# Attention then mixture of depths: the tail scores move to second place in the slot, the squares are summed a slot later, and the gate rows go ahead of those sums

## The chip, the cores and the metric

One NeuronCore of a Trainium2 chip runs the whole program. The metric is the device time of one execution in microseconds (us). Each run below has a time, and the profiled execution also has a trace.

## The reference

The input is q, k, v of 8 batches, 12 heads, 448 tokens and 64 dimensions in float32, and a small mixture-of-depths layer behind the attention:

```
q_n = q / (norm(q) + 1e-6);  k_n = k / (norm(k) + 1e-6)
attn = softmax(q_n @ k_n.T / tau)            # tau = 0.1
x[b] = heads of (attn @ v) side by side      # 448 x 768
scores = x @ w_gate                          # one number per token
top = the 128 tokens of each batch with the largest scores
out = x;  out[top] += sigmoid(scores[top]) * (relu(x[top] @ w1) @ w2)
```

w1 is 768 x 1024 and w2 is 1024 x 768.

## The kernel before

**Pairs and slots.** Two heads make a pair, six pairs a batch, so there are N = 48 pairs. The loop `for i in range(N + 1)` has one slot for each pair. The schedule is manual: on each engine, instructions run in the order in which the program writes them, and the framework adds the waits. Tokens are cut into seven blocks of 64 for either head; keys are cut into three whole column groups for each head (c = 0, 1, 2) and one shared tail group (c = 3).

**What a slot does.** `scores(i, c)` multiplies into a PSUM tile `sc` (a pool of two tiles, each of two banks); `exps(i, c)` is the exponential of it on ACT. `pv_tails` and `pv` multiply the exponentials of the pair before with its values into `o_ps`; `pv_evac` divides by the sum and writes into `x_b`, the batch's x. `transposes(i+1)` brings the next pair's normalized q and k through PE into `qkT_ps`, and `qkT_copy` (DVE) copies them to SBUF: the next slot's scores read that copy. `scale(i+2)` (POOL) normalizes the pair after that into `qkn`, of which there is one, and `values(i+2)` casts its v.

**Norms.** `square(p)` (ACT) squares q and k of pair p, which arrive by DMA into one of four raw buffers; eight matmuls with the identity (`sum_pe`) fold the squares into the second bank of an `sc` tile, and `sum_dve` reduces them into `ss`. `norm_a` (three small ACT instructions) and `norm_b` (a DVE reciprocal) follow once for up to three pairs. Before, squares, their sums and the tail scores all lie in the last part of one slot: the tail scores use the first bank of the tile whose second bank holds the sums.

**Order before.** scores 0 and 1, `pv_tails`, `pv` | exps 0 and 1, squares | list D1 | `pv_evac` | lists A, D2 | scores 2, transposes, `qkT_copy` | sums on PE, scores 3, sums on DVE | exps 2 and 3, norms | list C, scale, values, list P2, list B.

**The second layer.** Its steps are put in lists by slot (`at(slot, where, ...)`). For batch b, from slot s = 6(b+1): `store_x` (two stores of x on the SP queue, and a casting DMA on the POOL queue that makes `xh`, x in bf16), four `gate` rows (DVE, x times w_gate with a running sum), `rank_prep` (POOL), `rank_rep` (PE), four `rank_count` rows and four `pick` (DVE), `select`, `gather` in two parts (PE, reads `xh`), `ffn1` and `ffn2` in two halves, and `scatter` (an indirect DMA that adds into out). `x_b` and `xh` have two buffers each, so batch b+2 writes where batch b was. The last batch's second layer runs behind the loop.

## Time and profile before

| what | value |
|---|---|
| times of the runs shown | 325.1 and 320.91 us, median 323.0 us |
| profiled execution | 323.22 us |
| its span, first to last instruction | 319.3 us |
| mean granted TensorE clock | 0.897 of full |
| 48 slots, tail exponential of slot 0 to that of slot 47 | 17.9 us to 285.6 us |
| stores of one batch's x, two transfers | 768 and 576 KB |

The span is what the trace shows; about 3.9 us of the profiled execution's time lie outside it. PE, DVE, ACT, POOL and SP are the engines; PEld is PE's weight load.

### The profile page before, as it was taken

What the parts mean: (1) busy time and instruction counts of PE and PEld (TensorE: products, weight loads), DVE (VectorE), ACT (ScalarE), POOL (GpSimd) and SP (SyncE); (2) the same over time, 40 slices, a digit from 0 to 9 for tenths busy, and PEclk for the clock granted to TensorE, in tenths of its full rate; (3) what the DMA queues carried; (4) which work ended last, traced back from release to release, by engine and by line L of the source; (5) the groups of instructions that cost most, each with busy time, mean ns of one, the idle gap of its engine ahead of it and who ended that gap; (6) DMA issues with size and microseconds to landing.
All of it is one profiled execution on the core that took longest, in us unless ns stands there. A gap on an engine that the chain in (4) does not pass through costs nothing.

```text
span 319.3 us, 10375 instructions
## 1 busy us (share of the span) xinstructions
PE 246.7 (77%) x4503; PEld 188.9 (59%) x4503; DVE 184.1 (58%) x476; ACT 206.8 (65%) x317; POOL 158.1 (50%) x183
## 2 busy tenths in 40 slices
PE   7678777769897886969798789877978789587370
PEld 7466545547765675647665677656756566464350
DVE  2334365585667573667557575767674767686120
ACT  4768998968786785667667688755865646452020
POOL 5542657753667352844558357725572437303201
PEclk9989999997999697987889799959995979699697
DMA  7899999999999699667959499949121570306533
GB/s 271 228 302 290 280 268 247 293 284 275 291 282 256 142 226 240 202 123 162 235 150 271 84 220 251 270 89 206 32 28 26 132 142 2 51 2 134 139 49 49
DMA packets 31805, 57.68 MB, mean 181 GB/s; under 512 B 2192, under 2 KB 27792, under 8 KB 30736
## 3 DMA queue, kind: packets, MB, share of 16 engines
q1 hardware_dynamic: 27216, 43.75, 51.5%
q0 software_dynamic: 4128, 12.58, 21.8%
q8 instruction: 35, 0.57, 0.8%
q10 hardware_dynamic: 416, 0.69, 0.6%
q14 instruction: 10, 0.08, 0.1%
HBM read 39.71 MB, written 14.16 MB: 169 GB/s over the span
## 4 chain that ended last, share of the span: by engine, by line
PE 41%; DVE 24%; ACT 17%; DMA 8%; issue 5%; SPq 2%; POOLq 1%; DVEq 0%; ACTq 0%
PE o_ps L316 9%; PE sc L276 7%; ACT expS L289 7%; DVE junk L350 6%; PE m_ps L461 5%; PE sc L200 5%; DMA qk_raw<-in_k_dram 5%; ACT sq L193 4%; PE m_ps L470 4%; ACT expS L292 4%; DVE junk L395 4%; DMA xh<-x_b 4%; DVE qkT L264 3%; DVE x_b L330 3%; PE qkT_ps L258 3%
## 5 line engine op out<-in xcount | busy, mean ns | idle before, releaser
L231 POOL TENSOR_TENSOR qkn<-qk_raw,rs 128x896 bf16<-128x896 f32 (+1 forms) x48 | 92.3, 1922 | 117.3 <-PE qkT_ps L258 94.0
L289 ACT ACTIVATE expS<-sc 128x896 bf16<-128x896 f32 x144 | 126.4, 913 | 26.9 <-PE sc L276 26.9
L276 PE MATMUL sc<-qkT 64*128 64x448 bf16 x288 | 51.9, 387 | 33.0 <-DVE qkT L264 24.6
L292 ACT ACTIVATE expS<-sc 128x448 bf16<-128x448 f32 x48 | 26.1, 543 | 47.6 <-DVE ss L206 47.1
L316 PE MATMUL o_ps<-vo,expS 128*128 128x65 bf16 x1152 | 49.2, 202 | 0.0
L193 ACT ACTIVATE sq<-qk_raw 128x896 bf16<-128x896 f32 x48 | 45.5, 951 | 2.7 <-DMA qk_raw<-in_k_dram 2.7
L276 PEld LDWEIGHTS <-qkT 64*128 64x128 bf16 x288 | 13.8, 95 | 52.2 <-DVE qkT L264 29.1
L316 PEld LDWEIGHTS <-expS 128*128 128x128 bf16 x1152 | 42.9, 103 | 2.9
L200 PE MATMUL sc<-sq,iden_b 128*128 128x112 bf16 x384 | 29.3, 226 | 12.6 <-ACT sq L193 12.6
L258 PEld LDWEIGHTS <-qkn 64*64 64x64 bf16 x1344 | 28.2, 117 | 15.6 <-issue 12.2
L258 PE MATMUL qkT_ps<-iden_b,qkn 64*64 64x64 bf16 x1344 | 34.3, 203 | 3.8 <-POOL qkn L231 1.9
L264 DVE COPY qkT<-qkT_ps 128x960 bf16<-128x960 bf16 x48 | 31.4, 655 | 8.2 <-PE qkT_ps L258 7.9
L330 DVE TENSOR_TENSOR x_b<-o_ps,rden 128x512 f32<-128x512 f32 x48 | 33.2, 691 | 1.7
L329 DVE RECIPROCAL rden<-o_ps 128x8 f32<-128x8 f32 x48 | 9.9, 207 | 41.2 <-PE o_ps L316 37.9
L350 DVE CUSTOM_DVE_ANT_0 junk<-x_b,wg_b 128x768 bf16<-128x768 f32 (+1 forms) x32 | 33.4, 1045 | 0.2
L200 PEld LDWEIGHTS <-iden_b 128*128 128x128 bf16 x384 | 24.2, 105 | 14.1 <-issue 12.1
L238 POOL CAST vo<-v_raw 128x448 bf16<-128x448 f32 x48 | 28.6, 598 | 0.0
L461 PEld LDWEIGHTS <-w_sb 128*128 128x128 bf16 x384 | 24.9, 104 | 5.1 <-issue 3.6
L461 PE MATMUL m_ps<-xeT,w_sb 128*128 128x128 bf16 x312 | 22.2, 233 | 3.0 <-issue 2.4
L395 DVE SCALAR_TENSOR_TENSOR junk<-m_ps,own,tie 128x448 bf16<-128x448 f32 (+1 forms) x32 | 21.9, 683 | 0.8
L485 POOL DMA_INDIRECT out_dram<-oe,idx x8 | 13.0, 1630 | 18.6 <-DVE oe L435 8.8
L221 DVE RECIPROCAL rs<-rs 128x42 f32<-128x42 f32 (+2 forms) x18 | 7.0, 387 | 24.7 <-ACT rs L216 20.3
(83 smaller groups left out, 278.6 us busy)
## 6 DMA issues: line engine op xcount, KB each, us to landing
qk_raw<-in_q_dram SPq DMA_DIRECT2D x15, 672.0 KB, 4.8
qk_raw<-in_k_dram SPq DMA_DIRECT2D x15, 672.0 KB, 14.3
out_dram<-x_b SPq DMA_DIRECT2D x8, 768.0 KB, 10.8
xh<-x_b POOLq DMA_DIRECT2D x8, 768.0 KB, 12.4
v_raw<-in_v_dram SPq DMA_DIRECT2D x30, 192.0 KB, 11.4
out_dram<-x_b SPq DMA_DIRECT2D x8, 576.0 KB
v_raw<-in_v_dram SPq DMA_DIRECT2D x30, 144.0 KB, 8.7
w_sb<-in_moe_w_dram POOLq DMA_DIRECT2D x2, 1536.0 KB, 21.3
```

The source lines that it names most:

```text
L193: nc.scalar.activation(sq_tiles[p], raw[gi % NRAW][0][:, :, g].rearrange("p a b d -> p a (b d)"), AF.Square)
L200: nc.tensor.matmul(out=dst, lhsT=iden_b, rhs=sq[:, :, s * D8:(s + 1) * D8], start=(s == 0), stop=(s == Dh // D8 - 1))
L231: eng.tensor_mul(kn[:, :, b0:b1], qk[:, :, g, b0:b1], rs[:, m, :, b0:b1].rearrange("p a (b o) -> p a b o", o=1) .to_broadcast([P, 2, b1 - ...
L258: nc.tensor.transpose(out=qkT_ps[r, o:o + T], in_=kn[r, a, s], identity=iden_b[r, r], tile_position=(u * T, u * T))
L264: nc.vector.tensor_copy(qkT_tiles[p], qkT_ps[:, :W])
L276: nc.tensor.matmul(out=sc[:, u, :S], lhsT=qkT[r, KO + c * P:KO + (c + 1) * P], rhs=qkT[r, :S], start=True, stop=True, tile_position=(u * D ...
L289: nc.scalar.activation(ex[:, 2 * c:2 * c + 2], sc[:, :, :S], AF.Exp, scale=inv_tau)
L292: nc.scalar.activation(ex[:, TAIL], sc[:, 0, :S], AF.Exp, scale=inv_tau)
L316: nc.tensor.matmul(out=o_ps[:, u, j * E:(j + 1) * E], lhsT=ex[:, 2 * c + u, qc(j)], rhs=vo[:, u * NS + c], start=False, stop=(c == NC - 1) ...
L330: nc.vector.tensor_mul(x_tiles[b][:, :, 2 * hp * Dh:2 * (hp + 1) * Dh] .rearrange("p j (u d) -> p j u d", u=2), o[:, :, :, :Dh], rden.to_b ...
L350: nc.vector.tensor_tensor_reduce(out=junk[:, d0:d1], in0=x_tiles[b][:, j, d0:d1], in1=wg_b[:, d0:d1], scale=1.0, scalar=0.0 if prev is Non ...
L461: nc.tensor.matmul(out=ps[:, f * CAP:(f + 1) * CAP], lhsT=w1_sb[:, t, fc * P:(fc + 1) * P], rhs=xeT[:, t], start=(t == 0), stop=(t == KD - 1))
```

## The change

The slot's order becomes: list P1 | scores 0, `pv_tails` | scores 3 together with the PE sums of the squares made in the *last* slot | exps 0 and 3, this slot's squares | list D1 | sums on DVE, some norms | `pv`, `pv_evac` | list A | scores 1, exps 1, scores 2, exps 2, transposes, `qkT_copy` | scale, values, lists P2 and C, the other norms, list D3, list B. So four `sc` tiles are still taken in a slot, in another order. Squares are made six pairs ahead instead of five, with three buffers for `sq`.

Gate rows move from D2, behind `pv_evac`, to D1, ahead of the sums. Two of four `rank_count` rows and all four `pick` go from ahead of `qkT_copy` to D3, behind it. Most steps of the second layer start one slot later. `store_x` no longer makes `xh`: `half_x` does, five slots later (four and three for batches 5 and 6), at the slot's start.

At the end, slot 48 is no longer a loop pass: the last pair's `pv` stands behind the loop. The last pair's x goes into a tile of its own, `x_last`; `half_x` for the other five sixths of the last batch is issued in slot 47, and ACT casts the last sixth. `gather` part 1 and both `ffn1` halves of batch 6 run there too. At the start, the loads of group 3's q and k go ahead of the v loads of group 2 on the SP queue. `xeT` and `hT` become separate tiles for each half.

The core of the diff:

```
-    for gi in range(3):
-        load(gi, 2, nc.sync)
+    load(0, 2, nc.sync)
+    load(1, 2, nc.sync)
+    load(3, 0, nc.sync)
+    load(3, 1, nc.sync)
+    load(2, 2, nc.sync)
+    load(3, 2, nc.sync)
...
+    def half_x(b, d1=D):
+        xh_tiles[b] = xp.tile([P, NS, D], BF16, name="xh")
+        nc.gpsimd.dma_start(out=xh_tiles[b][:, :, :d1], in_=x_tiles[b][:, :, :d1])
...
+    late = dict(gate=(1, 2, 3, 4), rep=5, half=5, rank=6, select=7,
+                ffn=((8, "B"), (9, "B"), (10, "B"), (11, "A")))
+    mid = dict(late, ffn=((8, "B"), (9, "A"), (9, "B"), (10, "A")))
+    early = dict(gate=(1, 1, 2, 3), rep=4, half=4, rank=5, select=6,
+                 ffn=((7, "B"), (8, "A"), (8, "B"), (9, "A")))
+    last = dict(gate=(1, 1, 2, 2), rep=3, half=3, rank=4, select=5, ffn=())
...
+        at(s, "P2", store_x, b)
         for j in range(NS):
-            at(s + m["gate"][j], "D2", gate, b, j)
-        at(s + m["prep"], "P2", rank_prep, b)
+            at(s + m["gate"][j], "D1", gate, b, j)
+        at(s + m["gate"][3], "P2", rank_prep, b)
+        at(s + m["half"], "P1", half_x, b)
...
+        run(i, "P1")
+        sq = SQ.get(i - 1, [])
+        scores(i, 0)
+        if prev:
+            pv_tails(i - 1)
+        sc = ps_sc.tile([P, 2, 512], FP32, name="sc")
+        scores(i, 3, sc)
+        sums(sq, sc)
+        exps(i, 0)
+        exps(i, 3)
+        for p in SQ.get(i, []):
+            square(p)
+        run(i, "D1")
+        sums_dve(sq, sc)
+        norms(sq, i, True)
+        if prev:
             pv(i - 1)
-        if live:
-            exps(i, 0)
-            exps(i, 1)
-            for p in SQ.get(i, []):
-                square(p)
-        run(i, "D1")
-        if prev:
             pv_evac(i - 1)
         run(i, "A")
-        run(i, "D2")
...
+        scores(i, 1)
+        exps(i, 1)
+        scores(i, 2)
+        exps(i, 2)
         if nxt:
             transposes(i + 1)
             qkT_copy(i + 1)
-        if live:
-            sc = ps_sc.tile([P, 2, 512], FP32, name="sc")
-            sums(SQ.get(i, []), sc, lambda: scores(i, 3, sc))
-            exps(i, 2)
-            exps(i, 3)
-            norms(SQ.get(i, []))
-        run(i, "C")
         if i + 2 < N:
             scale(i + 2)
             values(i + 2)
         run(i, "P2")
+        run(i, "C")
+        norms(sq, i, False)
+        run(i, "D3")
...
         run(i, "B")
...
+    gather(b, 1, "A", True)
+    store_x(bb, x_last, 5 * P, D)
...
+    ffn1(b, 0, "A", True)
+    rank_prep(bb, True)
     ffn1(b, 1, "A", True)
-    rank_prep(bb)
+    nc.scalar.activation(xh_last, x_last, AF.Copy)
+    rank_rep(bb)
```

## Rows read from the trace of the kernel before

**Rows 1.** Slots 29-34, 35-40, 41-46: length, busy PE, PEld, DVE, ACT, POOL; clock, DMA.

```profile
170.30:202.70 32.40, 27.81 (x552) 21.55 (x551) 22.03 (x57) 25.07 (x38) 19.23 (x21) 0.95 0.86 201
202.70:240.90 38.20, 30.08 (x556) 22.74 (x555) 27.13 (x70) 25.12 (x38) 22.16 (x23) 0.90 0.55 111
240.90:279.80 38.90, 30.76 (x529) 22.80 (x527) 25.00 (x58) 21.89 (x35) 16.83 (x18) 0.81 0.35 68
```

**Rows 2.** Waits over the span: total us, times, longest us.

```profile
ACT expS L292 <- DVE ss L206: 47.1, 43, 3.6
PE sc L276 <- DVE qkT L264: 24.6, 13, 3.7
PE sc L200 <- ACT sq L193: 12.6, 28, 1.2
```

**Rows 3.** Timeline of a slot with rank rows (slot 29), DVE and PE.

```profile
175.40 0.84 DVE L403 TENSOR_SCALAR sel<-iota_r,rank 128x128 bf16<-128x128 bf16 x4
176.27 0.66 DVE L264 COPY qkT<-qkT_ps 128x960 bf16<-128x960 bf16 x1
...
176.98 0.36 PE L276 MATMUL sc<-qkT 64*128 64x448 bf16 x2 [2.43 <-DVE qkT L264]
```

**Rows 4.** Timeline of ACT, tail exponentials of slots 4, 5, 6, 28 and 29.

```profile
38.02 0.54 ACT L292 ACTIVATE expS<-sc 128x448 bf16<-128x448 f32 x1 [0.33 <-DVE ss L206]
42.16 0.54 ACT L292 ACTIVATE expS<-sc 128x448 bf16<-128x448 f32 x1 [0.33 <-DVE ss L206]
47.05 0.54 ACT L292 ACTIVATE expS<-sc 128x448 bf16<-128x448 f32 x1 [0.33 <-DVE ss L206]
...
170.27 0.54 ACT L292 ACTIVATE expS<-sc 128x448 bf16<-128x448 f32 x1 [0.63 <-DVE ss L206]
177.14 0.54 ACT L292 ACTIVATE expS<-sc 128x448 bf16<-128x448 f32 x1 [2.57 <-DVE ss L206]
```

**Rows 5.** The chain that ended last, in order of time: start, us, what.

```profile
15.29 7.01 DMA qk_raw<-in_k_dram
22.39 0.96 ACT sq L193
...
289.17 11.57 DMA xh<-x_b
300.79 2.75 PE sc L447 x24
```

**Rows 6.** Timeline of PE through slot 32, which has one ffn1 half.

```profile
187.98 0.55 PE L276 MATMUL sc<-qkT 64*128 64x448 bf16 x4
...
191.00 0.55 PE L200 MATMUL sc<-sq,iden_b 128*128 128x112 bf16 x8 [0.63 <-ACT sq L193]
...
191.58 1.50 PE L461 MATMUL m_ps<-xeT,w_sb 128*128 128x128 bf16 x24
193.01 0.55 PE L276 MATMUL sc<-qkT 64*128 64x448 bf16 x4
```

**Rows 7.** Gate rows: their source line (ns min/median/max), and one beside POOL's scale.

```profile
L350 DVE CUSTOM_DVE_ANT_0 junk<-x_b,wg_b x32: 682/948/2320, 45.1 to 281.1; 128x768 bf16<-128x768 f32 x28, 128x512 bf16<-128x512 f32 x4
251.02 1.93 POOL L231 TENSOR_TENSOR qkn<-qk_raw,rs 128x896 bf16<-128x896 f32 x1 [3.40 <-PE qkT_ps L258]
...
251.44 2.32 DVE L350 CUSTOM_DVE_ANT_0 junk<-x_b,wg_b 128x768 bf16<-128x768 f32 x1
```

**Rows 8.** Timeline behind the loop: eight gather matmuls in slot 47, the last pick.

```profile
283.79 0.61 PE L447 MATMUL m_ps<-sel,xh 128*128 128x128 bf16 x8
...
296.66 0.26 DVE L403 TENSOR_SCALAR sel<-iota_r,rank 128x128 bf16<-128x128 bf16 x1
```

**Rows 9.** Timeline of POOL's rank_prep in slot 27, its first and last instruction.

```profile
166.17 1.04 POOL L358 TENSOR_TENSOR diag<-iden_x,gate 128x512 f32<-128x512 f32 x1
...
168.22 0.19 POOL L367 CAST sg<-r 128x4 bf16<-128x4 f32 x1
```

**Rows 10.** The casting DMA's source line: issue to landing of its eight, min/median/max.

```profile
DMA to landing us min/median/max: 8.5/12.4/14.1
```

More of the change, by code (lines that the diff above doesn't have):

```diff
@@ L321 @@
     x_tiles = {}
+    x_last = const.tile([P, NS, P], FP32)
+    xh_last = const.tile([P, NS, P], BF16)
     def pv_evac(i):
@@ L358, in rank_prep @@
         nc.gpsimd.tensor_mul(
-            diag, iden_x,
-            g.rearrange("p (j o) -> p j o", o=1).to_broadcast([P, NS, P]))
+            diag[:, :2 if split else NS], iden_x[:, :2 if split else NS],
+            g[:, :2 if split else NS].rearrange("p (j o) -> p j o", o=1)
+            .to_broadcast([P, 2 if split else NS, P]))
+        if split:
+            for j in (2, 3):
+                nc.scalar.activation(diag[:, j], iden_x[:, j], AF.Copy,
+                                     scale=g[:, j:j + 1])
         sg = moe.tile([P, NS, 3], BF16, name="sg")
@@ L440, in gather @@
         sel, xh = st[b]["sel"], xh_tiles[b]
-        if part == 0:
-            st[b]["xeT"] = moe.tile([P, KD, CAP], BF16, name="xeT")
         t0, t1 = ((0, cut), (cut, KD))[part]
+        xe = moe.tile([P, t1 - t0, CAP], BF16, name=f"xeT{part}_{t1 - t0}")
+        st[b].setdefault("xeT", []).extend(xe[:, t] for t in range(t1 - t0))
         ps = bank(big)
         for t in range(t0, t1):
+            src = xh if not (b == B - 1 and t == KD - 1) else xh_last
+            d0 = 0 if src is xh_last else t * P
             for j in range(NS):
                 nc.tensor.matmul(out=ps[:, (t - t0) * CAP:(t - t0 + 1) * CAP],
-                                 lhsT=xh[:, j, t * P:(t + 1) * P], rhs=sel[:, j],
+                                 lhsT=src[:, j, d0:d0 + P], rhs=sel[:, j],
                                  start=(j == 0), stop=(j == NS - 1))
-        evac(eng, st[b]["xeT"][:, t0:t1].rearrange("p t c -> p (t c)"),
-             ps[:, :(t1 - t0) * CAP], AF.Copy)
+        evac(eng, xe.rearrange("p t c -> p (t c)"), ps[:, :(t1 - t0) * CAP], AF.Copy)
     def ffn1(b, part, eng="D", big=False):
         xeT = st[b]["xeT"]
-        if part == 0:
-            st[b]["hT"] = moe.tile([P, KF, CAP], BF16, name="hT")
+        h = moe.tile([P, 4, CAP], BF16, name=f"hT{part}")
+        st[b].setdefault("hT", []).extend(h[:, t] for t in range(4))
         ps = bank(big)
@@ L498, in run @@
             fn(*args)
-    late = dict(gate=(0, 1, 2, 3), prep=3, rep=4, rank=5, select=6, gather=7,
-                ffn=((7, "B"), (8, "B"), (9, "B"), (10, "A")), scatter=10)
-    mid = dict(late, ffn=((7, "B"), (8, "A"), (8, "B"), (9, "A")), scatter=9)
-    early = dict(gate=(0, 0, 1, 2), prep=2, rep=3, rank=4, select=5, gather=6,
-                 ffn=((6, "B"), (7, "A"), (7, "B"), (8, "A")), scatter=8)
-    last = dict(gate=(0, 0, 1, 1), prep=1, rep=2, rank=3, select=4, gather=5,
-                ffn=((5, "B"),), scatter=None)
+    late = dict(gate=(1, 2, 3, 4), rep=5, half=5, rank=6, select=7,
[4 more added lines that the diff above has]
+    last = dict(gate=(1, 1, 2, 2), rep=3, half=3, rank=4, select=5, ffn=())
     for b in range(B - 1):
@@ L521 @@
         at(s + m["select"], "B", gather, b, 0)
-        at(s + m["gather"], "A", gather, b, 1)
+        if b < B - 2:
+            at(s + m["select"] + 1, "A", gather, b, 1)
         for (d, w), (fn, n) in zip(m["ffn"], ((ffn1, 0), (ffn1, 1), (ffn2, 0), (ffn2, 1))):
             at(s + d, w, fn, b, n)
-        if m["scatter"]:
-            at(s + m["scatter"], "P2", scatter, b)
+            if fn is ffn2 and n == 1:
+                at(s + d, "P2", scatter, b)
     bb = B - 1
@@ L529 @@
     gb = const.tile([P, NS], FP32)
+    gc = const.tile([P, NS], FP32)
     for j in range(NS):
-        at(N - 2, "D2", gate, bb, j, 0, 4 * P, None, ga)
-        at(N - 1, "D2", gate, bb, j, 4 * P, 5 * P, ga, gb)
-    for b in range(B - 1):
-        at(HP * (b + 1), "P2", store_x, b)
+        at(N - 3, "D1", gate, bb, j, 0, 2 * P, None, ga)
+        at(N - 1, "D1", gate, bb, j, 2 * P, 4 * P, ga, gb)
+        at(N - 1, "D3", gate, bb, j, 4 * P, 5 * P, gb, gc)
+    at(N - 1, "P2", half_x, bb, 5 * P)
+    at(N - 1, "P2", store_x, bb, None, 0, 5 * P)
     at(3, "D1", load_wg)
@@ L549, in warm, with sums, sums_dve, norms @@
                              start=True, stop=True)
-    def sums(ps, sc, tail=None):
+    def sums(ps, sc):
         for m, p in enumerate(ps):
             sum_pe(p, sc[:, 1, m * SW:(m + 1) * SW])
-        if tail:
-            tail()
+    def sums_dve(ps, sc):
         for m, p in enumerate(ps):
             sum_dve(p, sc[:, 1, m * SW:(m + 1) * SW])
-    def norms(ps):
+    def norms(ps, i=None, early=None):
         for p in ps:
             n, g = nplace[p]
-            if g == NORMS[n][1] - 1:
+            if g == NORMS[n][1] - 1 and (i is None or early == (NORMS[n][0] == i + 2)):
                 norm_a(n)
@@ L583 @@
     values(1)
-    for which in range(3):
-        load(3, which, nc.sync)
     for i in range(N + 1):
@@ L658 @@
     ps = [bank(True), bank(True)]
-    for h in range(2):
-        for n in range(2):
-            ffn2_mm(bb, n, ps[n], h * 4, h * 4 + 4)
+    ffn2_mm(bb, 0, ps[0], 0, KF)
+    ffn2_mm(bb, 1, ps[1], 0, KF)
     ffn2_evac(bb, 0, ps[0], "A")
```

56 lines of the change are left out of this document (25 added, 31 removed).

## Prediction

> **What bounds the kernel now.** I read the stretches first, for which engine is full; then the waits, for what stops it; then the timeline of single slots. In the undisturbed stretch of six slots PE is busy 27.8 of 32.4 us, ACT 25.1, DVE 22.0 [rows 1]. None is full, so the slot is a chain that goes round the engines with PE as its longest part. The reader is to see that three waits recur [rows 2]: the tail exponential waits for the sums' reduction on DVE (43 of 48 slots, 47.1 us), the scores wait for the copy of q and k (24.6 us in 13 waits), and the sums wait for the squares (12.6 us in 28). The first is no bound by itself: it is ACT's idle time, and the scores ask for little more. The second is PE's and dear: in slot 29, which has the rank rows, the picks and then the copy stand on DVE one behind the other, and PE waits 2.43 us [rows 3]. That slot lasts 6.87 us, 170.27 to 177.14 [rows 4]. Behind the loop, the chain is one transfer: 11.57 us of casting DMA, then the gather [rows 5].
>
> Slots without the second layer are short: 4.14 us from 38.02 to 42.16, and 4.89 to 47.05 when the norms' three small instructions follow [rows 4].
>
> **The change, part by part.** Every gain is counted against the profiled execution: 323.2 us, of which 319.3 are its span. It lies 0.2 us above the median of the runs, so I take nothing off for that.
>
> *Start.* The k load issued at 15.29 landed at 22.30, and a square stood waiting until 22.39 [rows 5]. Its issue stood behind twelve v loads; four of them now come after it. Four twelfths of the 15.3 us before it are at most some 4 us of earlier issue, and behind the load stands ACT, which has its own work until close to then. I take 2 us; ends 0 and 4.
>
> *Light slots (2 to 10).* The sums no longer wait for the squares of their own slot, but the transposes are now the last PE work, so that the copy lies open: 0.66 us [rows 3] plus two hand-overs. PE's own work for a slot follows from slot 32: 193.01 − 187.98 = 5.03, less 0.63 of waiting for the squares, less the ffn1 half (1.43 from its start at 191.58 to the next scores) leaves 2.97 [rows 6]. So 2.97 + 0.66 + about 0.4 of hand-overs = 4.0 us, against 4.14 and, every third slot, 4.89, where part of the norms comes under the copy. I take 0.2 us a slot, nine slots: 2 us; ends −1 and 4. This is the first place where a wait takes the other's place: the copy's for the square's.
>
> *Slots with the second layer, batches 0 to 3 (slots 11 to 34).* In a rank slot two rank rows and all picks go behind the copy. PE's 2.43 us of waiting then shrinks to the copy's own 0.71, which stays open as nothing else is on PE: 1.7 us for a batch [rows 3]. The spilled DVE work (the picks alone 0.84) lies in the next slot beside scores and pv. The squares' wait is 12.6 / 28 = 0.45 us [rows 2], four such slots a batch: 1.8 us. Against it, the second score pair's tile is free only when the sums are reduced, and this now stands behind a gate row (0.95, [rows 7]): walked by hand through slot 32, the reduction ends 0.3 us after PE wants the tile. So 4 × 0.15 = 0.6 us remain. Together 2.3 us a batch, 9.2 in four; ends 1.0 and 3.5 a batch.
>
> *Slots 35 to 40.* They take 38.2 us where the undisturbed six take 32.4 [rows 1]. Two of them are rank slots: 3.4 us. In the gate slot a second row met POOL's scale and took 2.32 instead of 0.95 us right ahead of the copy; ahead of the sums it has PE's pv as cover. With that and the squares' 0.6, I take 5.4; ends 3.4 and 7.
>
> *Slots 41 to 46.* 38.9 us at a clock of 0.81, PE busy 30.8 [rows 1]. The gate rows go two to a slot here, with the same collision (row at 251.44, [rows 7]), and one rank slot follows. One ffn1 half also goes behind the loop. PE's busy time is what it can't go below, so at most 8 us; the rank slot and two blocked rows are 1.7 + 2 × 1.4 = 4.5. I take 6; ends 3 and 8.
>
> *Behind the loop.* The big transfer leaves one slot earlier and is five sixths as long: issued some 4.6 us before 289.17, 9.6 us long, it lands near 294.2. Then the last pick is late next: 296.66 + 0.26 = 296.9 [rows 8]. The gather started at 300.79 [rows 5], so 3.9 us. The two ffn1 halves, ffn2 and gather part 1 of batch 6 fill what was idle, so PE comes to the gather without a pause: eight such matmuls took 0.61 at the higher clock [rows 8], 24 would be 1.8 in place of 2.75 us, 0.9 more. Two of four diag blocks move to ACT, beside POOL: nothing, as the two run at once. I take 5; ends 2 and 6.
>
> Gains: 2 + 2 + 9.2 + 5.4 + 6 + 5 = 29.6 us.
>
> *What is added: x's buffer.* `half_x` reads x_b five slots later than before, and batch b+2's first `pv_evac` writes the same buffer two slots after it. On POOL the transfer stands behind scale, values and rank_prep (166.17 to 168.41, 2.2 us [rows 9]), so it leaves near the end of the transposes of its slot, about 10 us ahead of that write by clean slot lengths. Landings took 8.5 to 14.1 us, median 12.4 [rows 10], all with 1.4 MB of stores beside them that now went five slots before. Behind the waiting `pv_evac` on DVE stands the q and k copy, and for that PE waits. So 0 to 4 us in each of five batches (0 to 4); I take 1, nearer the short end for the missing stores: 5 us; ends 0 and 20.
>
> *Loads a slot earlier.* Squares need q and k one slot sooner while buffers come free at the same time. Only the start showed ACT waiting for them. I take 1.5 us; ends 0 and 4. Three `sq` buffers, separate xeT and hT halves: nothing, and they take waits away at most; what covers them is PE's order. `half_x` and the stores stand past nothing on SP that waits; the scatter goes one slot later on POOL beside idle time.
>
> *Gate rows against POOL.* At the slot's start POOL runs scale and values; in the middle, where the rows were, it mostly waits for transposes. A row begun inside scale ended 0.8 us after scale did (251.44 + 2.32 against 251.02 + 1.93, [rows 7]): it stood still until scale was through. In slots with an ffn half, DVE's evacuation comes first and the row starts about when scale ends. So I take 1 us in all; the far end is the rival below.
>
> The Trainium skill, "SBUF — State Buffer", section "Who interferes with whom", says that a DVE instruction with two SBUF inputs and a GpSimd instruction that reads SBUF take turns on one port pair and the second blocks in full. This trace agrees: 2.32 us in place of 0.95. It speaks against moving the rows to where scale runs; by it alone the rival's sum holds.
>
> Costs 7.5, so 323.2 − 29.6 + 7.5 = 301.1: **301 us**.
>
> **The rivals.**
>
> *Buffer wait in full* (0.15). Every `pv_evac` two slots after `half_x` waits 4 us: five times 4 in place of 1 is 301 + 15 = 316. For it: the median landing is longer than the 10 us available, and DMA is busy through the first batches. Against: the stores are gone from beside it.
>
> *The wait only moves* (0.13). The reduction gates the second score pair as it gated the tail exponential, and the open copy eats the rest; only the start and the end gain: 323 − 7 = 316. For it: both waits lie on the same `sc` tile, and DVE's order decides both. Against: two rank rows and four picks really leave the copy's way.
>
> *Gate rows on the path* (0.12, slower). Each full row starts inside scale, and the sums, the second score pair, the transposes and the copy follow it. Extra 1.37 us (2.32 − 0.95), 28 rows [rows 7]: 38 us, or 301 + 38 = 339; where 0.3 us a row stays covered, 331. It decides once the blocked row ends later than pv and the first score pair do. For it: scale starts when transposes end and DVE is free 0.7 us later. Against: in ffn slots DVE first waits for the ffn half.
>
> **How the numbers follow.** The forecast has 0.60, with its own range 289 to 311: the low end takes the gains with no cost (293.6) and a third of what their upper ends (43.0 in all) add to 29.6; the high end gives up ten of the 18 us that lie between the gains taken and their lower ends (11.4 in all). The range 289 to 318 adds most of both rivals at 316 and leaves out the slower one and the outskirts. Two per cent (about what a measurement here can tell from none) are below 316.5 or above 329.5. Faster: 0.60, half of each rival at 316: 0.74. Same: the other halves, 0.14. Slower: 0.12.
>
> **What would show it.** In the trace after: the tail exponential starts right behind the first, with no wait for the reduction; the sums don't wait for squares; the rank slots take about 5 us; scores wait for the copy some 0.7 us in slots without an ffn half. If the buffer rival holds, `rden` or `x_b` on DVE waits for the casting DMA in the slots 13, 19, 25, 31 and 37. If gate rows do, many of 28 show 2.3 us and the second scores wait for the reduction. Behind the loop, the gather waits for the last pick and not for a DMA. The prediction is wrong if PE's waits for DVE grow by more than the copy's.

## The result and the profile after

The changed kernel takes 287.97 us (two runs, 287.29 and 288.65) against 323.0 us: 0.892 of the time before, 95% interval 0.865 to 0.918. Run again later it took 290.56 us, 0.908 (0.896 to 0.920). The forecast of 301 us had the direction and lies 13 us too high; its range began at 289, so the time is 1 us under it.

The profiled execution took 288.65 us, 1.8 us of it outside its span of 286.9. The trace of before is not that of the execution of 323.22 us: the record gives that one a span of 321.4 us at a clock of 0.892, and the trace has 319.3 at 0.897. So 1.8 us lie outside the span before as well, not 3.9, and the two traces are 32.4 us apart where the medians are 35.0 apart. First the page's head and the busy time of each engine in the whole span, before and then after.

```profile
span 319.3 us, 10375 instructions
...
PE 246.7 (77%) x4503; PEld 188.9 (59%) x4503; DVE 184.1 (58%) x476; ACT 206.8 (65%) x317; POOL 158.1 (50%) x183
```

```profile
span 286.9 us, 10402 instructions
...
PE 230.8 (80%) x4503; PEld 174.2 (61%) x4503; DVE 181.3 (63%) x482; ACT 208.4 (73%) x322; POOL 150.7 (53%) x183
```

The reader is to see that PE runs the same 4503 matmuls in 15.9 us less, at a granted clock of 0.957 instead of 0.897. Its idle time went from 319.3 − 246.7 = 72.6 to 56.1 us, 16.5 less. So the span's 32.4 us are half waits and half the same work done in less busy time.

The stretches below run from the first exponential of slot 11, 17, 23, 29, 35, 41 and 47 to the next of them. Columns as in [rows 1].

```profile
65.64:96.84 31.20, 27.32 (x545) 20.90 (x544) 21.30 (x56) 24.83 (x39) 17.01 (x21) 0.89 1.06 278
96.84:126.17 29.33, 26.79 (x553) 20.05 (x552) 22.03 (x58) 25.02 (x39) 18.04 (x22) 1.00 0.94 223
126.17:157.07 30.90, 27.88 (x553) 20.96 (x552) 22.02 (x58) 25.13 (x39) 17.33 (x22) 0.94 0.93 221
157.07:187.80 30.73, 27.18 (x552) 20.06 (x550) 22.34 (x58) 25.03 (x38) 18.08 (x22) 1.00 0.94 221
187.80:220.72 32.92, 28.86 (x565) 21.21 (x564) 23.07 (x61) 25.46 (x38) 19.56 (x28) 1.00 0.62 135
220.72:252.75 32.03, 25.39 (x521) 18.54 (x520) 24.69 (x67) 20.79 (x34) 18.43 (x21) 1.00 0.53 101
```

The table has the same marks in the trace before, each the timeline's start of a slot's first exponential, and splits each gain into PE's idle and PE's busy time:

| stretch | before: us, PE busy | after: us, PE busy | gain | of it PE idle | PE busy | forecast, before costs |
|---|---|---|---|---|---|---|
| start to slot 11 | 66.14, 49.78 | 65.64, 47.35 | 0.5 | −1.9 | 2.4 | 4 |
| slots 11 to 34, batches 0 to 3 | 137.51, 116.51 | 122.16, 109.17 | 15.4 | 8.0 | 7.3 | 9.2 |
| slots 35 to 40 | 37.76, 29.54 | 32.92, 28.86 | 4.8 | 4.2 | 0.7 | 5.4 |
| slots 41 to 46 | 41.41, 32.12 | 32.03, 25.39 | 9.4 | 2.7 | 6.7 | 6 |
| slot 47 and behind the loop | 36.48, 18.75 | 34.15, 20.04 | 2.3 | 3.6 | −1.3 | 5 |
| span | 319.3, 246.7 | 286.9, 230.8 | 32.4 | 16.5 | 15.9 | 29.6 (less 7.5 of costs) |

So the middle gave 30 us and both ends nearly nothing. No stretch of six slots is over 32.9 us now, and PE's granted clock is 1.00 in four of six. Before, two of the four stretches in slots 11 to 34 were long, and slots 41 to 46 too, all at a low clock:

```profile
98.61:135.08 36.47, 29.97 (x558) 22.78 (x556) 22.27 (x58) 25.23 (x39) 19.21 (x21) 0.86 0.85 209
135.08:171.20 36.12, 30.73 (x558) 23.62 (x556) 22.52 (x58) 25.24 (x39) 18.83 (x21) 0.86 0.78 192
...
241.41:282.82 41.41, 32.12 (x546) 24.21 (x547) 27.95 (x66) 22.30 (x37) 16.83 (x18) 0.81 0.33 64
```

PE's busy time in the first two was 30.0 and 30.7 us at 0.86, and is 26.8 and 27.9 at 1.00 and 0.94, for nearly as many matmuls. Slots 41 to 46 went from 32.1 us (0.81) to 25.4 (1.00); one ffn1 half left them too.

The waits of after, of those that [rows 2] lists and what answers to them:

```profile
DVE ss L210 <- ACT expS L296: 24.5, 14, 3.4
...
PE sc L280 <- DVE qkT L268: 15.6, 14, 3.5
...
PE sc L280 <- DVE ss L210: 7.2, 12, 0.9
...
ACT expS L296 <- PE sc L204: 5.1, 7, 1.3
```

The tail exponential no longer waits for the reduction (47.1 us before) but in seven cases for the sums on PE; the sums' wait for the squares (12.6 us) is gone from the list. The first is now the other way round: the reduction waits for the tail exponential (24.5 us, DVE's idle time), and PE for the reduction, 7.2 us in 12 waits. All of PE's waits for DVE together even rose, from 29.5 to 36.4 us; those for ACT fell from 21.0 to 4.3 and those for a DMA from 6.6 to 1.4 (sums over the view's lines).

A slot that has the spilled rank rows and picks reads as follows (timeline, DVE and PE).

```profile
105.63 0.66 DVE L268 COPY qkT<-qkT_ps 128x960 bf16<-128x960 bf16 x1 [0.18 <-PE qkT_ps L262]
106.35 0.36 PE L280 MATMUL sc<-qkT 64*128 64x448 bf16 x2 [0.76 <-DVE qkT L268]
...
107.66 0.81 DVE L416 TENSOR_SCALAR sel<-iota_r,rank 128x128 bf16<-128x128 bf16 x4
...
108.38 0.95 DVE L358 CUSTOM_DVE_ANT_0 junk<-x_b,wg_b 128x768 bf16<-128x768 f32 x1
...
109.37 0.28 DVE L210 TENSOR_REDUCE ss<-sc 128x14 f32<-128x112 f32 x1
...
109.70 0.37 PE L280 MATMUL sc<-qkT 64*128 64x448 bf16 x2 [0.60 <-DVE ss L210]
...
110.72 0.65 DVE L268 COPY qkT<-qkT_ps 128x960 bf16<-128x960 bf16 x1
```

The copy comes 0.18 us behind the transposes, and PE waits 0.76 us for it, not 2.43 [rows 3]. The picks, the gate row and the reduction then pass one behind the other while PE has tail products, scores and pv, and the reduction is late by 0.60 us. From copy to copy the slot takes 110.72 − 105.63 = 5.09 us; the rank slot before took 6.87 [rows 4]. Some executions of each kernel are disturbed and longer, so the ratios below are of undisturbed ones alone and the medians of all, and the profiled executions of e4, e7 and e8, which were disturbed, are used only where another run shows the same.

### The profile page after: what moved, and what is told of

The parts are those of the page before. It is cut to its first block, busy times and chain, and to the rows that moved or that the text cites. A ratio compares the mean times of both kernels' runs of the same rounds, so it can differ in the third digit from the quotient of the medians.

```text
span 286.9 us, 10402 instructions
## 1 busy us (share of the span) xinstructions
PE 230.8 (80%) x4503; PEld 174.2 (61%) x4503; DVE 181.3 (63%) x482; ACT 208.4 (73%) x322; POOL 150.7 (53%) x183
## 3 DMA queue, kind: packets, MB, share of 16 engines
q0 software_dynamic: 4512, 12.45, 24.5%
## 4 chain that ended last, share of the span: by engine, by line
PE 41%; DVE 21%; ACT 16%; DMA 10%; issue 7%; POOL 2%; SPq 1%; POOLq 1%; DVEq 0%; ACTq 0%
ACT expS L293 8%; PE sc L280 8%; DMA qk_raw<-in_k_dram 6%; PE o_ps L320 6%; PE m_ps L483 5%; DVE junk L408 5%; PE qkT_ps L262 5%; DVE junk L358 4%; DMA xh<-x_b 4%; PE sc L204 4%; PE m_ps L475 4%; ACT sq L197 3%; PE m_ps L462 3%; PE sc L285 3%; POOL qkn L235 2%
## 5 line engine op out<-in xcount | busy, mean ns | idle before, releaser
L235 POOL TENSOR_TENSOR qkn<-qk_raw,rs 128x896 bf16<-128x896 f32 (+1 forms) x48 | 80.7, 1681 | 101.0 <-PE qkT_ps L262 44.0
L280 PE MATMUL sc<-qkT 64*128 64x448 bf16 x288 | 49.3, 368 | 28.8 <-DVE qkT L268 15.6
L320 PE MATMUL o_ps<-vo,expS 128*128 128x65 bf16 x1152 | 46.3, 197 | 0.0
L268 DVE COPY qkT<-qkT_ps 128x960 bf16<-128x960 bf16 x48 | 31.4, 655 | 12.5 <-PE qkT_ps L262 12.5
L262 PEld LDWEIGHTS <-qkn 64*64 64x64 bf16 x1344 | 25.4, 111 | 15.8 <-issue 11.0
L358 DVE CUSTOM_DVE_ANT_0 junk<-x_b,wg_b 128x768 bf16<-128x768 f32 (+1 forms) x32 | 33.3, 1040 | 0.2
L262 PE MATMUL qkT_ps<-iden_b,qkn 64*64 64x64 bf16 x1344 | 30.8, 196 | 2.1 <-POOL qkn L235 2.1
L242 POOL CAST vo<-v_raw 128x448 bf16<-128x448 f32 x48 | 32.0, 668 | 0.0
L210 DVE TENSOR_REDUCE ss<-sc 128x14 f32<-128x112 f32 x48 | 12.7, 272 | 29.6 <-ACT expS L296 24.5
L204 PE MATMUL sc<-sq,iden_b 128*128 128x112 bf16 x384 | 28.0, 222 | 0.0
L475 PEld LDWEIGHTS <-w_sb 128*128 128x128 bf16 x384 | 22.3, 99 | 3.2 <-issue 2.2
L498 POOL DMA_INDIRECT out_dram<-oe,idx x8 | 13.0, 1628 | 14.5 <-DVE oe L448 7.0
L475 PE MATMUL m_ps<-xeT,w_sb 128*128 128x128 bf16 x288 | 18.1, 219 | 1.6 <-DVE xeT L446 1.6
```

The costliest lines, as they stand in the source:

```text
L204: nc.tensor.matmul(out=dst, lhsT=iden_b, rhs=sq[:, :, s * D8:(s + 1) * D8], start=(s == 0), stop=(s == Dh // D8 - 1))
L235: eng.tensor_mul(kn[:, :, b0:b1], qk[:, :, g, b0:b1], rs[:, m, :, b0:b1].rearrange("p a (b o) -> p a b o", o=1) .to_broadcast([P, 2, b1 - ...
L242: nc.gpsimd.tensor_copy(vo_bufs[p % NB][:, :, :Dh], raw[gi % NRAW][1][:, g])
L262: nc.tensor.transpose(out=qkT_ps[r, o:o + T], in_=kn[r, a, s], identity=iden_b[r, r], tile_position=(u * T, u * T))
L280: nc.tensor.matmul(out=sc[:, u, :S], lhsT=qkT[r, KO + c * P:KO + (c + 1) * P], rhs=qkT[r, :S], start=True, stop=True, tile_position=(u * D ...
L320: nc.tensor.matmul(out=o_ps[:, u, j * E:(j + 1) * E], lhsT=ex[:, 2 * c + u, qc(j)], rhs=vo[:, u * NS + c], start=False, stop=(c == NC - 1) ...
```

## The experiments

Each ran beside the kernel before, whose median in these jobs was 318.9 to 321.7 us. "Six slots" is the shortest of the four batches 0 to 3, from the start of one pair's transposes to that of the sixth pair after it (pairs 12 to 18, 18 to 24, 24 to 30, 30 to 36, read off the timeline). It is the clean batch, free of a pause or a late load. "Pairs 0-5", "5-12" and "41-47" are the time between those pairs' transposes. PE busy and clock are those of the span, and "at 0.50" is the time in it for which the granted clock was at its lower level, 1.2 GHz.

| run | median, us | ratio, 95% | pairs 0-5 | 5-12 | six slots | 41-47 | PE busy | clock | at 0.50, us |
|---|---|---|---|---|---|---|---|---|---|
| before | 323.0 | | 26.9 | 31.4 | 32.45 | 42.0 | 246.7 | 0.897 | 66 |
| after | 287.97 | 0.892 (0.865-0.918) | 30.1 | 28.5 | 29.33 | 31.9 | 230.8 | 0.957 | 24 |
| e1 | 312.86 | 0.972 (0.962-0.983) | 28.8 | 30.5 | 31.84 | 40.7 | 241.5 | 0.906 | 59 |
| e2 | 309.96 | 0.968 (0.957-0.978) | 28.2 | 31.4 | 32.23 | 33.5 | 239.1 | 0.944 | 35 |
| e3 | 320.52 | 1.000 (0.994-1.006) | 29.3 | 30.0 | 31.67 | 42.3 | 243.8 | 0.901 | 62 |
| e14 | 314.99 | 0.988 (0.981-0.995) | 28.7 | 30.5 | 32.94 | 35.7 | 239.7 | 0.902 | 61 |
| e5 | 301.53 | 0.952 (0.944-0.959) | 31.5 | 28.1 | 32.28 | 33.2 | 237.9 | 0.910 | 55 |
| e6 | 294.39 | 0.931 (0.919-0.942) | 28.7 | 29.9 | 28.67 | 33.3 | 235.7 | 0.935 | 38 |
| e10 (after again) | 290.56 | 0.908 (0.896-0.920) | 31.4 | 28.1 | 29.32 | 31.6 | 235.8 | 0.930 | 40 |

**One part alone in the kernel before.** e1: the tail exponentials go ahead of the reduction.

```
+    def sums_dve(ps, sc):
         for m, p in enumerate(ps):
             sum_dve(p, sc[:, 1, m * SW:(m + 1) * SW])
...
             exps(i, 2)
             exps(i, 3)
+            sums_dve(SQ.get(i, []), sc)
             norms(SQ.get(i, []))
```

> The kernel before with one swap: the third and the tail exponential are issued ahead of the sums' reduction on DVE, so that the tail exponential can't wait for it (47.1 us of waiting in the trace of before). Theory A (the prediction's: that wait is idle time of ACT and bounds nothing but light slots): 0.3 us in some nine light slots and little more, 317 to 323 us. Rival (the wait sits on the chain in most slots, as the next slot's second score pair needs that tile): 0.3 to 0.7 us in 43 slots, 295 to 310 us.

The tail exponential lost its wait for the reduction (it now waits 8.1 us for scores, 16 times) and the time fell by 2.8%. Yet the copy's wait is where it was, and the reduction now waits for the exponential, as in after:

```profile
PE sc L276 <- DVE qkT L264: 24.8, 14, 3.7
DVE ss L206 <- ACT expS L292: 21.1, 26, 4.4
```

A clean batch is 0.6 us shorter; the four batches together (pairs 12 to 36) take 131.9 us for 137.5, most of it out of the two long stretches. Neither side fits: the prediction's "no bound by itself" allowed little more than nothing, and its rival 0.3 to 0.7 us in 43 slots.

e2: two rank rows and the picks go behind the copy.

```
-            at(s + m["rank"], "D1" if j < 2 else "D2", rank_count, b, j)
+            at(s + m["rank"], "D1" if j < 2 else "D3", rank_count, b, j)
...
-            at(s + m["rank"], "D2", pick, b, j)
+            at(s + m["rank"], "D3", pick, b, j)
...
         norms(SQ.get(i, []))
+        run(i, "D3")
```

> The kernel before with two of the four rank rows and the four picks of each of seven batches moved behind the copy of q and k. Theory A (the prediction's price): 1.7 us in each of seven rank slots, 12 us, so about 311 us. Rival (a stall of 2.4 us also lowers the clock of the slots behind it, and the slot after it is long as well): 2.5 to 3.5 us each, 298 to 306 us. Against both: the work only moves to the next slot's reduction, 320 to 325 us.

3.2% faster, but nearly all of it at the end: pairs 41 to 47 fell from 42.0 to 33.5 us, where the two rank slots went from 8.01 to 4.98 and from 7.78 to 4.39. A clean batch gained 0.2 us: the rank slot is 0.9 shorter, the next 0.9 longer. There the selection on PE, early in the slot, waits for the picks that moved into it:

```profile
PE sc L276 <- DVE qkT L264: 9.8, 7, 2.4
...
PE m_ps L412 <- DVE sel L403: 7.6, 6, 1.5
```

So the same move was worth 3.0 and 3.4 us at the end of the loop and nothing in the steady part: the 1.7 us of the forecast fits neither.

e3: squares one slot earlier, summed in the next.

```
-        sq_tiles[p] = prep.tile([P, 2, NB7 * Dh], BF16, name="sq")
+        sq_tiles[p] = prep.tile([P, 2, NB7 * Dh], BF16, name="sq", bufs=3)
...
-        SQ.setdefault({3: 0, 4: 0, 5: 1, 6: 1}.get(p, p - 5), []).append(p)
+        SQ.setdefault({3: 0, 4: 0, 5: 1, 6: 1, 7: 2, 8: 2}.get(p, p - 6), []).append(p)
...
-            sums(SQ.get(i, []), sc, lambda: scores(i, 3, sc))
+            sums(SQ.get(i - 1, []), sc, lambda: scores(i, 3, sc))
...
-            norms(SQ.get(i, []))
+            norms(SQ.get(i - 1, []))
```

> The kernel before with the squares made one slot earlier and summed in the slot after, in the old order of the slot. Theory A: it takes away the sums' wait for the squares, 12.6 us in 28 slots, part of which something else takes over: 310 to 317 us. Rival (PE's wait for the squares only stands in for its wait for the copy): 320 to 324 us.

The wait for squares is gone, and no time with it. A clean batch gained 0.8 us (the forecast had 0.6), but the copy's wait rose from 24.6 to 29.2 us, scores wait for exponentials, and the start took 29.3 us instead of 26.9:

```profile
PE sc L276 <- DVE qkT L264: 29.2, 13, 3.7
...
PE sc L276 <- ACT expS L289: 8.0, 12, 2.8
```

e4 puts the three edits into the kernel before together, in its old order.

> The three edits of the runs beside it together in the kernel before: exponentials ahead of the reduction, squares a slot earlier, two rank rows and the picks behind the copy; slot order, gate rows, the casting transfer and the end stay. If the gain of the whole change comes from these waits, this has most of its 32 us apart from the end's 2 to 3: 293 to 300 us. If it comes from the new slot order itself (tail scores second, two score pairs with the transposes) or from the casting transfer standing apart from the stores, it stays above 305 us.

316.06 us, 0.987 (0.979 to 0.994): the three together give less than e2 alone, and likely less than e1, whose interval just meets this one. The parts don't add in the old order; what makes them pay is to be looked for in what e4 leaves out, the new order first.

**One part undone in the changed kernel.** e5: the rank rows and picks go ahead of the copy again.

```
         run(i, "A")
+        run(i, "D3")
...
-        run(i, "D3")
```

> The changed kernel with two rank rows and the picks back ahead of the copy of q and k (the last slot's four small gate rows move with them). If the rank slots are the main source: 1.7 to 3 us in each of seven slots, 300 to 309 us. If the new order covers them elsewhere: 288 to 292 us.

301.53 us, 11 us above the changed kernel's second run. A clean batch is back at 32.28 us, which is that of before: in a clean batch, all that the new order has hangs on this one place. The timeline shows how: the copy stands behind the four picks and PE waits longer than it did before, since no sums and tail scores lie behind the transposes any more.

```profile
107.59 1.48 DVE L416 TENSOR_SCALAR sel<-iota_r,rank 128x128 bf16<-128x128 bf16 x4
...
109.10 0.66 DVE L268 COPY qkT<-qkT_ps 128x960 bf16<-128x960 bf16 x1
...
109.82 0.56 PE L280 MATMUL sc<-qkT 64*128 64x448 bf16 x2 [3.45 <-DVE qkT L268]
```

e6: the 28 gate rows of batches 0 to 6 go behind `pv_evac`, as before.

```
-            at(s + m["gate"][j], "D1", gate, b, j)
+            at(s + m["gate"][j], "D2", gate, b, j)
...
         run(i, "A")
+        run(i, "D2")
```

> The changed kernel with the 28 whole gate rows back behind the last pair's evacuation, as before the change. If the rows ahead of the sums are a gain (no row right ahead of the copy): 291 to 300 us, with rows of 2.3 us ahead of the copy. If their place costs time (blocked behind POOL's scale, the reduction and the second score pair behind them): 280 to 286 us. Prediction's step: 1 us of cost for their place, 287 us.

294.39 us, 0.931 against 0.908 for the changed kernel run again; the intervals just meet, so the loss of some 4 us is likely and not shown. Six slots are even shorter (28.67 against 29.33): a row ahead of the reduction does cost a little there. It is repaid between pairs 5 and 12 (29.9 us against 28.1 and 28.5) and in the slots with two rows, of which two took 8.36 and 7.42 us for 5.04 and 5.52 in after. e9 takes both sides: rows of batches 0 to 4 behind, of 5 and 6 ahead.

```
-            at(s + m["gate"][j], "D1", gate, b, j)
+            at(s + m["gate"][j], "D2" if b < 5 else "D1", gate, b, j)
...
         run(i, "A")
+        run(i, "D2")
```

> The changed kernel with the gate rows of batches 0 to 4 (one to a slot) back behind the evacuation, those of batches 5 and 6 (two to a slot) staying ahead of the sums. If the rows ahead of the sums delay the reduction, and with it the second score pair, by some 0.5 us in one or two slots a batch: 2 to 4 us less than the unchanged kernel beside it. If they are better ahead everywhere: 2 to 6 us more.

290.74 us, 0.907 (0.897 to 0.918), which is the changed kernel's own. What a clean batch wins (28.81) is lost again between pairs 5 and 12 (29.9).

e7: the casting transfer goes out with the stores, five slots earlier, as before.

```
         at(s, "P2", store_x, b)
+        at(s, "P2", half_x, b)
...
-        at(s + m["half"], "P1", half_x, b)
```

> The changed kernel with the casting transfer back in the slot of the stores, right after them, four to five slots earlier. If the wait for x's buffer costs what was predicted (5 us): 283 us. If it costs nothing (the trace shows one wait of 0.7 us on DVE): 287 to 289 us. If the transfer beside the stores hurts (landing late, PE's pauses on nothing visible): 290 to 296 us.

295.56 us, 0.925 (0.910 to 0.941), which overlaps the changed kernel's interval: undoing the later transfer brings no gain, though no wait for x's buffer is left in its trace.

e14 is e5, e6 and e7 at once: new order, squares earlier, new start and end, and nothing else.

> The changed kernel with three parts undone: two rank rows and the picks ahead of the copy, the whole gate rows behind the evacuation, the casting transfer in the slot of the stores. What is left is the new slot order with the squares a slot earlier, and the start and end. If the order alone carries most of the gain: 296 to 304 us. If the order pays only together with the rank rows behind the copy: 308 to 318 us, 2 to 4 per cent below before.

314.99 us, 0.988: 1.2% for the order with its start and end, and a clean batch of 32.94 us, 0.5 more than before. The copy's wait is longer than in any kernel above:

```profile
PE sc L280 <- DVE qkT L268: 39.0, 20, 3.5
```

With e2 and e5 this makes a square. Rank rows behind the copy gain 3.2% in the old order. The new kernel with rank rows ahead gains 4.8% (e5), and only 1.2% when the gate rows and the transfer go back as well (e14). Both together (after) gain 9 to 11%. A clean batch changes by −0.2 us (e2), −0.2 (e5; +0.5 in e14) and −3.1 (after). So in the steady part the two pay only together, while over the whole time 3.2 and 4.8 already come to 8%.

**The start and the buffer.** e8 makes the squares of pairs 6, 8 and 18 one slot later, so that they wait less for their loads.

```
-        SQ.setdefault({3: 0, 4: 0, 5: 1, 6: 1, 7: 2, 8: 2}.get(p, p - 6), []).append(p)
+        SQ.setdefault({3: 0, 4: 0, 5: 1, 6: 2, 7: 2, 8: 3, 18: 13}.get(p, p - 6), []).append(p)
```

> The changed kernel with three squares moved one slot later (pairs 6, 8 and 18), where the trace after shows squares on ACT that wait for a k load (slots 1 and 12, waits of 1.5 and 2.7 us, the slots 9.2 and 7.6 us long). If those waits are what the earlier squares cost: 4 to 7 us less than the unchanged kernel beside it. Rival (the DMA engines are full, so the wait comes back at the next load): 0 to 2 us less.

291.34 us, 0.906 (0.892 to 0.919): nothing. The third slot took 9.18 us in the changed kernel and takes 5.08, but the fifth went from 5.90 to 10.23 (e16, which has the same edit: 4.80 and 8.38). The wait came back at the next load.

e10 is the changed kernel as it is, in the same job, and e11 is e8 and e9 together.

> The changed kernel as it is, for comparison on the same chip as the runs beside it: 286 to 292 us, with the long slots 2 and 13 in the same places if they come from loads, and any other long slot elsewhere if it comes from PE's pauses for nothing that the trace shows.

> The two edits beside it together in the changed kernel: three squares later, single gate rows behind the evacuation. If both hold and are apart, the sum of their gains: 279 to 283 us; if the rows behind the evacuation are worse, near the run with the squares alone.

290.56 and 290.33 us (0.912, 0.900 to 0.924). Neither edit nor both move the time.

e12: e8, with the loads of w1 and w2 in slots 7 and 10 in place of 3 and 6, to free the start.

```
-    at(3, "P2", load_w, w1_sb, ...)
-    at(6, "P2", load_w, w2_sb, ...)
+    at(7, "P2", load_w, w1_sb, ...)
+    at(10, "P2", load_w, w2_sb, ...)
```

> The changed kernel with three squares later (as two runs ago) and the two weight loads issued in slots 7 and 10 instead of 3 and 6. Theory (the first fourteen slots are bound by what the DMA engines bring, so a wait taken away at one load comes back at the next unless bytes leave that stretch): slots 4 and 5 lose the wait that went there, 4 to 6 us less than the unchanged kernel, 283 to 287 us, slot 47's end some 5 us earlier. Rival (the waits are each a matter of issue order): no change in the sum of slots 1 to 14, 289 to 292 us.

304.30 us, 0.949 (0.942 to 0.956), 13 us above e8, from which it differs by this alone. The start is no shorter (29.6 us). One slot, from pair 14's transposes to pair 15's, takes 22.94 us. The source lines of the weight loads, then of the casting transfer and its readers up to 120 us, and a line of the waits show why:

```profile
L182 POOL DMA_DIRECT2D w_sb<-in_moe_w_dram x2: 968/1018/1067, 55.0 to 68.8; - x2
```

```profile
L462 PEld LDWEIGHTS <-xh x24: 96/152/152, 93.5 to 99.3; 128*128 128x128 bf16 x24
...
L352 POOL DMA_DIRECT2D xh<-x_b x2: 564/575/586, 69.8 to 114.3; - x2
...
DMA to landing us min/median/max: 6.9/15.3/23.7
```

```profile
DVE x_b L338 <- issue: 16.8, 1, 16.8
```

w2's load leaves POOL's queue at 68.8 us, batch 0's cast at 69.8 behind it; it lands 23.7 us later, at 93.5, when the gather's first weights load. Batch 2's first write of x stood still for 16.8 us; the profile names no releaser for this wait, and e13, which gives x a third buffer on top, shows that it was for x's buffer. So the buffer rival's mechanism is real, and a weight load just ahead switches it on. Whether the order on the queue or the bytes in flight held the transfer up, no run separates.

```
-            x_tiles[b] = xp.tile([P, NS, D], FP32, name="x_b")
+            x_tiles[b] = xp.tile([P, NS, D], FP32, name="x_b", bufs=3)
```

> The run beside it with three buffers for x_b instead of two, so that no evacuation can wait for the casting transfer. If the buffer wait is what the traces show (0.7 to 2.4 us, in the first batch alone): 0 to 2 us less than the run beside it. If it costs in each batch, as the prediction took: 5 us less.

303.94 us, 0.951: no gain, because the gather needs the same bytes. DVE's wait went, and PE's came in its place at about the same length:

```profile
PE m_ps L462 <- DMA xh<-x_b: 17.1, 1, 17.1
```

e15 sends the q and k loads of group 4 ahead of group 3's v loads; e16 is that and e8.

```
     load(2, 2, nc.sync)
-    load(3, 2, nc.sync)
...
     values(1)
+    load(4, 0, nc.sync)
+    load(4, 1, nc.sync)
+    load(3, 2, nc.sync)
...
-            for which in range(3):
+            for which in range(2 if gi == 0 else 0, 3):
```

> The changed kernel with the q and k loads of group 4 ahead of the v loads of group 3 on the SP queue. Pair 5's transposes stand at 39.2 to 40.5 us in the changed kernel and at 36.1 before. If the order of the loads decides when squares stop waiting: the wait in slot 2 stays (group 3), the one in slot 4 goes, pair 5's transposes at 37 to 38 us and 1 to 2 us less than the unchanged kernel. If the bytes do: no change.

> The run beside it with three squares one slot later (pairs 6, 8 and 18) as well, so that slot 2 doesn't wait for group 3 and slot 4 not for group 4. If the order of the loads decides: pair 5's transposes at 34 to 36 us, 3 to 5 us less than the unchanged kernel (284 to 287 us). If the bytes do: 38 to 40 us again, 288 to 291 us.

290.71 and 290.31 us (0.905 and 0.904): no change. The start takes 29.0 and 29.4 us; in the changed kernel and all its variants it takes 28.7 to 31.8. No kernel here beats the changed one by more than its runs scatter.

## Why the prediction was right in direction and too small

*The tail exponential, the sums, the rank slot, the open copy: right.* All four signs came as named: no wait for the reduction, none for the squares, rank slots of 4.94 to 5.35 us in batches 1 to 3, and 0.76 us for the copy.

*PE's busy time: the step that failed.* The sum has terms for waits alone and holds PE's own work fixed. For slots 41 to 46 it says so: "PE's busy time is what it can't go below, so at most 8 us". That stretch gave 9.4 us, and 6.7 of them are PE's busy time (an ffn1 half that left it is some 1.5 us of this). Over the span the forecast was 29.6 less 7.5, or 22.1 us. PE's idle time fell by 16.5 us, so the waits were priced high, not low. Its busy time fell by 15.9 us, for which the sum had nothing. In the changed kernel's second run the two are 19.9 and 10.9.

The trace shows where this comes from: a stop of PE costs more than its own length. Here is the stop of [rows 3] and the stretch that begins 1.3 us behind it, then the longer stop that e5 brings back and what follows it (columns as in [rows 1]):

```profile
174.55:176.98 2.43, 0.00 (x1) 0.00 (x1) 2.33 (x10) 0.01 (x1) 1.15 (x2) 1.00 0.80 142
178.32:181.74 3.42, 3.42 (x70) 2.96 (x68) 2.50 (x9) 3.38 (x5) 0.48 (x1) 0.50 0.04 8
```

```profile
106.36:109.82 3.46, 0.01 (x3) 0.01 (x2) 3.36 (x10) 0.53 (x1) 2.18 (x2) 0.74 0.60 100
109.82:114.87 5.05, 5.05 (x83) 3.77 (x83) 2.27 (x8) 3.30 (x5) 0.00 (x0) 0.50 0.67 142
```

In the trace before, such a stretch at 0.50 begins in each of the seven rank slots, during the stop (2.03 to 3.67 us) or within 1.4 us of its end. Together they are 41 of the 66 us that this trace has at 0.50. e5 brings a stop of 2.6 to 3.8 us back into each of the seven, and such a stretch with each. The changed kernel's trace has 24 us at 0.50, and PE is busy in 17.7 of them, not in 53.3. At 0.50 the same work took 1.5 to 1.8 times as long as at 1.00: 28 transposes 0.95 us (at 180.16 before) for 0.63 (at 104.96 after), 24 gather matmuls 2.75 for 1.53. So 35.5 us less of it are an estimated 12 to 16 us of PE's busy time, and 15.9 were measured. The prediction read the clock of 0.81 in its rows and gave no term to its return.

That the stop alone brings the lower clock is not shown: in the changed kernel's second run three stretches at 0.50 (at 139, 170 and 200 us) have no stop of over 0.9 us in the 8 us ahead of them. Nor does the time go with the clock in step: e2 has 0.944 at 310 us, e10 0.930 at 290.6.

*Rank rows behind the copy: the wait right, its slot mis-sized.* The prediction put it as "PE's 2.43 us of waiting then shrinks to the copy's own 0.71 ...: 1.7 us for a batch", and added 0.6 for the squares. The wait went to 0.76 us, 1.67 less. But the two slots with rank rows fell from 7.67 + 4.99 = 12.66 us (pairs 30 to 32 before) to 4.94 + 5.03 = 9.97 (pairs 18 to 20 after), 2.7 less. A whole clean batch gained 32.45 − 29.33 = 3.1 us in place of 2.3. PE's idle time in it fell by 2.05 us (32.40 − 27.81 before, slots 29 to 34 [rows 1]; 29.33 − 26.79 after, slots 17 to 22), close to the forecast. Another 1.02 us are PE's busy time, at a clock of 0.95 before and 1.00 after.

What the prediction didn't see is that the new order needs this move. In it the sums and tail scores no longer stand behind the transposes, so rank rows ahead of the copy cost PE 3.45 us (e5). From there the move is worth 32.28 − 29.33 = 2.95 us a batch, in the old order 0.2 (e2). The squares' 0.6 was measured alone at 0.8 (e3).

*Slots 11 to 34.* Between the transposes of pairs 12 and 36 the time fell by 13.2 us, of which 12.5 are the four clean batches. The long slots between and beside them give little net: the trace before holds 137.5 − 4 × 32.45 = 7.7 us above four clean batches, the trace after 124.3 − 4 × 29.33 = 7.0. They are other ones, though. Before, PE stood still twice with nothing that the trace shows ahead of it:

```profile
123.02 0.40 PE L461 MATMUL m_ps<-xeT,w_sb 128*128 128x128 bf16 x4 [2.43 <-issue]
...
156.79 0.38 PE L258 MATMUL qkT_ps<-iden_b,qkn 64*64 64x64 bf16 x13 [1.66 <-issue]
```

After, the longest such stop is 1.2 us, and a late load and x's buffer (below) make the long slots. What stops PE so isn't settled.

*Slots 35 to 40: right* (4.8 for 5.4, nearly all of it idle time). *Slots 41 to 46: mis-sized*, 9.4 for 6, by the step that failed: of the waits only 2.7 us came, of PE's busy time 6.7. e2 alone takes 8.5 us out between pairs 41 and 47, 6.4 of it in the two rank slots.

*Light slots: mis-sized the other way.* Between pairs 5 and 12 they gained 2.9 us, 0.4 a slot where 0.2 was taken. By e6 and e9 (29.9 against 28.5) half of it is the place of batch 0's gate rows.

*The start: wrong.* A gain of 2 us was forecast (from four twelfths of 15.3 us, which are 5.1 and not 4) and 1.5 of cost for loads a slot earlier. From pair 0 to pair 5 it took 30.1 instead of 26.9 us, and ate the light slots' gain. One stall stands out:

```profile
20.63 0.95 ACT L197 ACTIVATE sq<-qk_raw 128x896 bf16<-128x896 f32 x1 [1.48 <-DMA qk_raw<-in_k_dram]
...
24.07 0.56 PE L280 MATMUL sc<-qkT 64*128 64x448 bf16 x2 [3.54 <-DVE qkT L268]
...
74.13 0.95 ACT L197 ACTIVATE sq<-qk_raw 128x896 bf16<-128x896 f32 x1 [2.69 <-DMA qk_raw<-in_k_dram]
```

A square waits 1.48 us for its load on ACT; the norms are behind it, then DVE's reciprocal, then the copy, then PE for 3.54 us. The same came back at 74.13. Squares earlier by themselves make the start longer (e3, 29.3); but e1 and e2, which leave the start alone, have 28.8 and 28.2, so some 1 to 2 us of the 3.2 are how loads happened to arrive. Moving the squares (e8), the v loads (e15) or the weights (e12) moved the stall and didn't shorten the start. That the arrival of the first loads sets it is argued from that, not shown.

*x's buffer: priced at 1 us in each of five batches, came in one.* DVE waited in one place, slot 13, in the first batch alone (timeline, then the landings of the casting DMA):

```profile
80.33 0.69 DVE L338 TENSOR_TENSOR x_b<-o_ps,rden 128x512 f32<-128x512 f32 x1 [0.75 <-DMA xh<-x_b]
```

```profile
DMA to landing us min/median/max: 5.6/8.3/11.4
```

In the changed kernel run again it is 2.40 us (the profile names no releaser there), PE stops for 2.41 us behind it, and 6.8 us at 0.50 begin in that stop. The slots from pair 13's to pair 15's transposes took 12.4 us in the first run, which has a late load there as well, and 14.5 in the second, where the same two slots of the next batch (pairs 19 to 21) took 9.5. So the one batch cost some 3 to 5 us, and the other four nothing. The transfers land in a median of 8.3 us in place of 12.4 [rows 10], inside the 10 us that the prediction had worked out. It took the missing stores as the reason to go near the short end. That reason isn't borne out: e7, whose casts go out beside the stores again, has a median of 9.3 us, between the 8.3 here and the 10.1 of the second run.

*Gate rows against POOL: right.* 28 full rows average 1103 ns, before 1096. By e6 their place ahead of the reduction costs 0.66 us a clean batch and saves 1.5 between pairs 5 and 12. Three are over 1.2 us, all in batch 0; the third, at 61.21, took 2.03:

```profile
49.08 2.03 DVE L358 CUSTOM_DVE_ANT_0 junk<-x_b,wg_b 128x768 bf16<-128x768 f32 x1
...
52.90 2.60 DVE L358 CUSTOM_DVE_ANT_0 junk<-x_b,wg_b 128x768 bf16<-128x768 f32 x1
```

The slower rival asked for 28 of them. It fails since scale is through when the row begins: in the slot shown scale ran from 105.74 for 1.68 us and the row began at 108.38; in a slot without rank rows, 208.11 for 1.69 and 210.71.

*Behind the loop: half.* 5 us were taken and 2.3 came, and the sign named (the gather waits for the last pick, not for a DMA) failed. The chain that ended last, then the last pick and the gather in the timeline:

```profile
257.59 12.10 DMA xh<-x_b
...
269.73 1.53 PE sc L462 x24
```

```profile
269.50 0.25 DVE L416 TENSOR_SCALAR sel<-iota_r,rank 128x128 bf16<-128x128 bf16 x1
269.73 1.29 PE L462 MATMUL sc<-sel,xh 128*128 128x128 bf16 x20 [1.37 <-DMA xh<-x_b]
```

Five sixths of the transfer took 12.1 us, not 9.6 (the whole took 11.57 before), so the term's scaling by length failed. The transfer lands at 269.69 and the pick ends at 269.75: neither alone could be shortened for gain. The 24 gather matmuls took 1.53 us for the 1.8 forecast.

*The rival "the wait only moves"* held for the wait itself: PE waits for DVE 36.4 us, 6.9 more than before, though its waits for the copy fell from 24.6 to 15.6; growth of that kind is what the prediction named as the sign against itself. It failed for the time, since PE's waits for ACT and DMA fell by 21.9 us and its busy time by 15.9.

## What to carry to other kernels

Before the stops of an engine are added up, look at the granted clock behind each of them: here a stop of 2.4 us was followed by 3.4 to 6.8 us at half the clock, and a sum over waits alone missed 15.9 us of busy time. Two reorderings that free the same copy must be priced in one walk through the new order: the wait that is left when only one is done is not the wait of the old trace (2.43 there, 3.45 here). Rank one's own parts by undoing each in the finished kernel as well as doing each in the old one; here one part was worth 0.2 us a clean batch in the old kernel and 2.95 in the finished one. Before a transfer is moved, look at what is issued just ahead of it: the same cast took 5.6 to 11.4 us in the changed kernel, and 23.7 behind a weight load on POOL's queue.
